# Expert tiles of 128 rows in place of 256, with three weight buffers and fetches three tiles ahead

## The chip, the core and the metric

The kernel runs on one core of a Trainium2 chip. The time is the device time of one execution in microseconds (us), from the first to the last instruction and what lies around them; a median of several runs is given. The profile is one execution recorded by the hardware profiler. Its engines are TensorE (PE for its matmuls, PEld for its weight loads), VectorE (DVE), ScalarE (ACT), GpSimd (POOL) and SyncE (SP), which here only issues transfers.

## What is computed

Two stages: attention between a sequence and a small state, per batch and head, and then a mixture of experts in which each of the 4352 rows goes to the one expert with the highest logit. Everything is float32.

```python
def _attn_ref(x, state):            # x (8, 8, 512, 64), state (8, 8, 32, 64)
    ...
    xread = np.matmul(a, state)     # a: softmax over the states
    ...
    sread = np.matmul(a2, x)        # a2: softmax over the tokens
    return np.concatenate([xread, sread], axis=2)

def _moe_ref(x, w_gate, w1, w2):    # x (4352, 512), w1 (8, 512, 1024), w2 (8, 1024, 512)
    logits = x @ w_gate
    expert_idx = np.argmax(logits, axis=1)
    ...
    for e in range(E):
        mask = expert_idx == e
        ...
        xe = x[mask]
        h = np.maximum(xe @ w1[e], 0.0)
        ye = h @ w2[e]
        out[mask] = gate_w[mask, None] * ye
```

## The kernel before

**Attention and routing** (up to about 214 us) goes over the eight batches. `route` (line 231) finds each row's expert and its rank there, and an indirect DMA of GpSimd (line 274) scatters the rows of x, each with its gate weight and its token number, into `xs_dram`, where every expert has a region of its own. Then VectorE computes tables (lines 344 to 388): for each tile the expert's number `eidx`, the rows of `xs_dram` to fetch `grow`, and which of its rows hold no token `inv_i`.

**Experts.** The rows of each expert are cut into tiles of T = 256 rows. A program has a fixed number of tiles, JT (line 49), enough for any split of 4352 rows over 8 experts: 24. All of them run, whatever the counts are; a tile past the last one fetches no rows, but does all the rest. The four steps of a tile j:

- `fetch(j)` (line 396): per 128 rows an indirect gather of GpSimd into one of six buffers `xg`; SP reads the expert's number and issues the loads of its w1 (2 MB) and w2 (2 MB) into `w1t` and `w2t`, tiles of `wpool` with two buffers each.
- `x_in(j)` (line 412): per 128 rows four transposes on TensorE into a PSUM tile `ptx`, evicted into `fxT` by ScalarE and VectorE in turn; VectorE also copies the gate weights `gw` and makes the row numbers `ti` of the output.
- `up(j)` (line 428): h = relu(x w1), with the weights as the stationary and `fxT` as the moving operand, 256 columns wide. Four PSUM tiles `ph` of 2 x 256 columns are evicted into `hT`, by ScalarE and VectorE in turn.
- `down(j)` (line 443): y = h w2, with `hT` stationary and 512 columns of w2 moving, once per 128 rows; VectorE multiplies by the gate weight into `y`, and an indirect DMA of GpSimd (line 452) scatters `y` into the output by `ti`.

The loop (line 462) writes up(j), x_in(j+1), down(j), fetch(j+2) for each j. From that a scheduler makes the order of each engine's instructions, and puts gathers and transposes whose buffers are free ahead of the first `up`. An engine takes its instructions in order, and waits on semaphores where an operand isn't ready or a buffer isn't free. So w1 of tile j+2 leaves when up(j) has read the last of its buffer, w2 when down(j) has. `wpool` is taken at the start of the kernel (line 53), beside the attention's pool `att`, which is released (line 390) ahead of the experts' pool `ffn`.

Of the kernel before, what the change touches and what calls it, by code (L numbers as in the profile page):

```python
# [9 lines left out]
FP32 = mybir.dt.float32  # L10
# [3 lines left out]
ALU = mybir.AluOpType  # L14
# [5 lines left out]
def kernel(  # L20
# [17 lines left out]
    SCALE = 0.125  # L38
    SO = S + NS                 # rows of one batch in the seam's token order
    NTOK = B * SO  # L40
    NC = S // 128               # token chunks of a batch; token s = 4 * p + c
    NPR = H // 2                # pairs of heads, 128 rows of (head, d)
    NDC = DM // 128
    NFC = F // 128
    XW = DM + 2                 # a routed row: x, gate weight, token number
    T = 256                     # tokens of one expert tile
    NH = T // 128
    # every split of NTOK tokens over E experts fits: sum of ceil(n_e / T)
    JT = (NTOK + E * (T - 1)) // T

    const = ctx.enter_context(tc.tile_pool(name="const", bufs=1))
    dram = ctx.enter_context(tc.tile_pool(name="dram", bufs=1, space=bass.MemoryType.DRAM))
    wpool = ctx.enter_context(tc.tile_pool(name="wpool", bufs=2))
    ps_m = ctx.enter_context(tc.tile_pool(name="ps_m", bufs=4, space=bass.MemoryType.PSUM))
    ps_o = ctx.enter_context(tc.tile_pool(name="ps_o", bufs=2, space=bass.MemoryType.PSUM))
    ps_s = ctx.enter_context(tc.tile_pool(name="ps_s", bufs=2, space=bass.MemoryType.PSUM))

    # expert e's rows start at e * NTOK, so that any split of the tokens fits
    xs_dram = dram.tile([E * NTOK, XW], I32)

# [1 line left out]
    ident = const.tile([128, 128], FP32)  # L62
# [7 lines left out]
                   allow_small_or_imprecise_dtypes=True)  # L70
    # 0/1 matrices and the one-hot rows are exact in bfloat16, and their products are counts
    U128 = const.tile([128, 128], BF16)
# [18 lines left out]

    # token numbers: batch b, chunk c, partition p -> b * SO + 4 * p + c
    tok_x = const.tile([128, B, NC], I32)
    nc.gpsimd.iota(tok_x[:], pattern=[[SO, B], [1, NC]], base=0, channel_multiplier=NC)
    # state rows of batches 4g..4g+3: partition 32 * i + n -> (4g + i) * SO + S + n
    quad = const.tile([128, 1], FP32)
# [13 lines left out]
    XB = 6  # L110
    # rows past an expert's count are not fetched: the buffers hold zeros or earlier rows there
    xg_bufs = []
# [7 lines left out]
    def evict(dst, src):  # L120
        """PSUM to SBUF, the two engines that can read PSUM in turn."""
        turn[0] += 1
        if turn[0] % 2:
            nc.scalar.copy(dst, src)  # L124
        else:
            nc.vector.tensor_copy(out=dst, in_=src)  # L126

    # =========================== attention and routing ===========================
    att = tc.alloc_tile_pool(name="att", bufs=2)

    # block-diagonal states: rows (h % 4, n), columns (h % 4, d), and their transposes by pairs
    bd = att.tile([128, B, 2, 4, D], FP32, bufs=1)
# [16 lines left out]
    def prep_state(b):  # L149
        pt = ps_m.tile([128, 2, 2, 128], FP32, tag="m", name="pt")  # L150
        for j in range(NPR):
            nc.tensor.transpose(pt[:, j // 2, j % 2, :], bd[:, b, j // 2, ts(j % 2, 2), :], ident[:])
        for i in range(2):
            evict(stT[:, b].rearrange("p (g i) n -> p g i n", i=2)[:, :, i, :], pt[:, :, i, ts(i, 2 * NS)])
        # state @ w_gate, by heads: the routing logits are the attention weights times it
        pg = ps_s.tile([128, 2, E], FP32, tag="s", name="pg")
        for j in range(NPR):
            nc.tensor.matmul(pg[ds(64 * (j % 2), 64), j // 2, :], lhsT=stT[:, b, j, :], rhs=wg[:, j, :],
                             start=True, stop=True, skip_group_check=True)
        evict(gst[:, b], pg[:])  # L160
# [10 lines left out]
    def read_weights(b, xT):  # L171
        """softmax over the states for every token"""
        a = att.tile([128, NC, H, NS], FP32, tag="a", name="a")
# [18 lines left out]
    def transpose_read(a):  # L192
        """rows (h % 4, n), columns tokens"""
        aT = att.tile([128, 2, NC, 128], FP32, tag="aT", name="aT")
        for g in range(2):
            pt = ps_m.tile([128, NC, 128], FP32, tag="m", name="pt")
            for c in range(NC):
                nc.tensor.transpose(pt[:, c, :], a[:, c, ts(g, 4), :], ident[:])
            evict(aT[:, g], pt[:])
        return aT  # L200

    def write_weights(b, xT):
        """softmax over the tokens for every state: rows (h % 4, n)"""
        a2 = att.tile([128, 2, S], FP32, tag="a2", name="a2")
# [16 lines left out]
    def transpose_write(a2):  # L221
        """rows tokens, columns (h % 4, n)"""
        a2T = att.tile([128, 2, NC, 128], FP32, tag="a2T", name="a2T")
        for g in range(2):
            pt = ps_m.tile([128, NC, 128], FP32, tag="m", name="pt")
            for c in range(NC):
                nc.tensor.transpose(pt[:, c, :], a2[:, g, ts(c, 128)], ident[:])
            evict(a2T[:, g], pt[:])
        return a2T

    def route(lg, row, tok, U):
        """lg: logits [128, U, E]; row: [128, U, XW] with x in place; sends each row to its expert's rows"""
        mx = att.tile([128, U, 1], FP32, tag="r_mx", name="r_mx")
        nc.vector.tensor_reduce(mx[:, :, 0], lg, AX.X, ALU.max)
        sh = att.tile([128, U, E], FP32, tag="r_sh", name="r_sh")
        nc.vector.tensor_tensor(sh[:], lg, mx[:].to_broadcast([128, U, E]), ALU.subtract)
        # the first expert among those at the maximum
        cand = att.tile([128, U, E], FP32, tag="r_cand", name="r_cand")
# [5 lines left out]
        nc.vector.tensor_tensor(oh[:], cand[:], m2[:].to_broadcast([128, U, E]), ALU.is_equal)  # L244
        # gate weight: exp(0) over the sum
        ex = att.tile([128, U, E], FP32, tag="r_ex", name="r_ex")
# [5 lines left out]
        nc.vector.tensor_copy(out=row[:, :, DM + 1:DM + 2].bitcast(I32), in_=tok.unsqueeze(2))  # L252
        # rank among the tokens of the same expert so far
        of = oh[:].rearrange("p u e -> p (u e)")
# [27 lines left out]
    def read_rows(b, aT):  # L282
        """x rows of the batch's tokens and their logits"""
        row = att.tile([128, NC, XW], FP32, tag="row", name="row")
# [15 lines left out]
    def write_rows(b, a2T):  # L300
        """x rows of the batch's states; those of four batches are routed together"""
        g4, r = b // 4, ds(NS * (b % 4), NS)
# [39 lines left out]

    # ============== tables: each tile's expert, its rows, and which of them are real ==============
    cnt = const.tile([128, E], FP32)
# [17 lines left out]
    nc.vector.tensor_copy(out=eidx[:], in_=ej[:])  # L362
    # the tile's number within its expert
    gt = const.tile([128, JT, E], FP32)
# [4 lines left out]
    nc.vector.tensor_scalar(loc[:], loc[:], float(T), iota_p[:, 0:1], ALU.mult, ALU.add)  # L369
    # the expert's count of tokens; far below zero for a tile past the last  # L370
    dcnt = const.tile([128, E], FP32)
# [19 lines left out]

    # ================================= experts =================================
    ffn = tc.alloc_tile_pool(name="ffn", bufs=2)
# [18 lines left out]
    def x_in(j):  # L412
# [3 lines left out]
        for k in range(NH):  # L416
# [4 lines left out]
            evict(xT[:, :, ts(k, 128)], pt[:])  # L421
            # no output row for a row that is not real: its token number is out of bounds
            nc.vector.tensor_tensor(ti[:, k:k + 1], xg[:, DM + 1:DM + 2].bitcast(I32),  # L423
# [4 lines left out]
    def up(j):  # L428
        xT, w1t = fs[j]["xT"], fs[j]["w1t"]
        hT = ffn.tile([128, NFC, T], FP32, tag="hT", name="hT")  # L430
        for f2 in range(NFC // 2):
            ph = ps_m.tile([128, 2, T], FP32, tag="m", name="ph")
            for i in range(2):
                for c in range(NDC):
                    nc.tensor.matmul(ph[:, i, :], lhsT=w1t[:, c, ts(2 * f2 + i, 128)], rhs=xT[:, c, :],  # L435
                                     start=(c == 0), stop=(c == NDC - 1), skip_group_check=True)
            if f2 % 2:
                nc.vector.tensor_scalar(hT[:, ts(f2, 2), :], ph[:], 0.0, None, ALU.max)  # L438
            else:
                nc.scalar.activation(hT[:, ts(f2, 2), :], ph[:], AF.Relu)  # L440
        fs[j]["hT"] = hT
# [17 lines left out]
    fetch(0)  # L459
    fetch(1)  # L460
    x_in(0)
    for j in range(JT):
        up(j)
        if j + 1 < JT:
            x_in(j + 1)
        down(j)
        if j + 2 < JT:
            fetch(j + 2)

    ffn.release()  # L470


# [28 lines left out]
```

## Time and profile before

| | |
|---|---|
| median of 3 runs | 931.94 us (928.96 to 932.76) |
| span of the profiled execution, first to last instruction | 925.5 us |
| mean granted TensorE clock | 0.979 of full speed |
| moved by DMA | 137.06 MB, 148 GB/s over the span |
| weight loads | 24 of w1 and 24 of w2, 2048.0 KB each |

No other time is recorded for the profiled execution than its span; the runs' median is 6.4 us above it. In the rows below, busy times are sums over an engine's instructions. Matmuls are pipelined, so the time of one is longer than the distance from one start to the next, and a price is read from starts. "idle before <- X" names what ended the idle time of the engine ahead of a group.

### The profile page before, as it was taken

The page shows a single profiled execution, that of the slowest core. Times are in us where ns is not written, and L with a number is a line of the kernel's source. Part 1 is how long each engine was busy: PE and PEld are TensorE (multiplying, and loading weights), DVE is VectorE, ACT ScalarE, POOL GpSimd, SP SyncE. Part 2 cuts the span into 40 slices and gives each one's busy share as a digit, 9 for nine tenths or more (in the row PEclk, how much of TensorE's full clock was granted, in tenths as well). Part 3 has the DMA queues.
Part 4 walks back from the last instruction along what each step waited for, and adds up shares of the span by engine and source line. Part 5 has one row for each costly group of instructions (what it writes and reads, how often), then busy time and mean ns, then how long its engine had stood idle before and what let it go on. Part 6 is the DMA issues. An engine that isn't in the chain of part 4 may idle for free.

```text
span 925.5 us, 9941 instructions
## 1 busy us (share of the span) xinstructions
PE 868.1 (94%) x4028; PEld 609.1 (66%) x4028; DVE 219.8 (24%) x628; ACT 99.4 (11%) x196; POOL 156.4 (17%) x166
## 2 busy tenths in 40 slices
PE   2999999990999999999999999999999999999997
PEld 2777877780766677666677666776667766667764
DVE  4456666543111111111111111111111111111110
ACT  1223322220100000000000000000000000000000
POOL 3022332224201111011110111111111101100000
PEclk9899999995799999999999999999999999999999
DMA  9034343117754464554544535545446435355300
GB/s 159 1 84 101 93 103 92 47 47 266 268 204 165 168 215 143 198 186 148 208 171 164 215 128 204 202 136 196 153 160 216 153 146 184 112 196 178 110 0 1
DMA packets 84061, 137.06 MB, mean 148 GB/s; under 512 B 40622, under 2 KB 40622, under 8 KB 84016
## 3 DMA queue, kind: packets, MB, share of 16 engines
q1 hardware_dynamic: 70912, 109.06, 36.5%
q0 software_dynamic: 10400, 26.83, 7.7%
q10 hardware_dynamic: 2704, 0.54, 0.4%
q8 instruction: 32, 0.52, 0.2%
q14 instruction: 13, 0.11, 0.0%
HBM read 122.22 MB, written 21.53 MB: 155 GB/s over the span
## 4 chain that ended last, share of the span: by engine, by line
issue 64%; POOL 9%; PE 3%; DMA 1%; POOLq 1%; DVE 0%
POOL out_dram L452 5%; POOL xg L398 3%; PE ph L435 2%; DMA xg<-xs_dram,grow 1%; PE py L448 1%; POOL xs_dram L274 0%; POOLq L398 0%; POOLq L452 0%; POOLq L496 0%; PE ptx L420 0%; DVE y L451 0%
## 5 line engine op out<-in xcount | busy, mean ns | idle before, releaser
L435 PE MATMUL ph<-fxT,w1t 128*128 128x256 f32 x1536 | 337.4, 381 | 0.0
L448 PE MATMUL py<-w2t,hT 128*128 128x512 f32 x768 | 333.6, 592 | 0.0
L435 PEld LDWEIGHTS ph<-fxT,w1t 128*128 128x128 f32 x1536 | 293.2, 191 | 50.1 <-issue 11.0
L448 PEld LDWEIGHTS py<-w2t,hT 128*128 128x128 f32 x768 | 144.2, 190 | 172.3 <-issue 172.2
L452 POOL DMA_INDIRECT out_dram<-y,ti x48 | 48.6, 1012 | 355.5 <-DVE y L451 323.9
L451 DVE TENSOR_SCALAR y<-py,gw 128x512 f32<-128x512 f32 x48 | 36.0, 751 | 293.6 <-PE py L448 293.6
L398 POOL DMA_INDIRECT xg<-xs_dram,grow x48 | 49.5, 1030 | 252.6 <-PE ptx L420 236.8
L440 ACT ACTIVATE hT<-ph 128x512 f32<-128x512 f32 x48 | 28.7, 597 | 553.0 <-PE ph L435 553.0
L438 DVE TENSOR_SCALAR hT<-ph 128x512 f32<-128x512 f32 x48 | 33.1, 690 | 145.9 <-PE ph L435 145.9
L420 PE MATMUL ptx<-ident,xg 128*128 128x128 f32 x192 | 27.7, 288 | 22.8 <-DMA xg<-xs_dram,grow 22.8
L274 POOL DMA_INDIRECT xs_dram<-row,r_sli x32 | 31.7, 992 | 81.7 <-DVE r_sli L271 30.2
L423 DVE TENSOR_TENSOR ti<-xg,inv_i 128x1 int32<-128x1 int32 x48 | 6.0, 158 | 164.8 <-DMA out_dram<-y,ti 143.0
L420 PEld LDWEIGHTS ptx<-ident,xg 128*128 128x128 f32 x192 | 23.6, 148 | 26.6 <-issue 22.8
L178 PE MATMUL pc<-stT,xT 128*128 128x64 f32 x256 | 37.2, 307 | 0.4 <-ACT stT L124 0.4
L178 PEld LDWEIGHTS pc<-stT,xT 128*128 128x128 f32 x256 | 34.9, 219 | 2.3 <-issue 1.4
L288 PE MATMUL px<-bd,aT 128*128 128x256 f32 x128 | 31.9, 387 | 0.1
L308 PE MATMUL pw<-x_nat,a2T 128*32 128x64 f32 x512 | 30.5, 219 | 0.0
L308 PEld LDWEIGHTS pw<-x_nat,a2T 128*32 128x32 f32 x512 | 28.8, 110 | 1.5 <-ACT r_ex L247 1.3
L189 POOL TENSOR_TENSOR a<-sh,sm 128x512 f32<-128x512 f32 x16 | 16.9, 1059 | 74.9 <-DVE sm L188 73.9
L167 PE MATMUL pt<-ident,x_nat 128*128 128x128 f32 x128 | 20.7, 300 | 7.4 <-DMA x_nat<-in_x_dram 6.8
L288 PEld LDWEIGHTS px<-bd,aT 128*128 128x128 f32 x128 | 22.7, 191 | 3.3 <-DVE aT L126 0.6
L124 ACT COPY fxT<-ptx 128x512 f32<-128x512 f32 x24 | 14.0, 585 | 98.3 <-PE ptx L420 98.3
(121 smaller groups left out, 391.0 us busy)
## 6 DMA issues: line engine op xcount, KB each, us to landing
w1t<-in_moe_w_dram SPq DMA_DIRECT2D x24, 2048.0 KB, 8.9
w2t<-in_moe_w_dram SPq DMA_DIRECT2D x24, 2048.0 KB, 9.1
x_nat<-in_x_dram SPq DMA_DIRECT2D x32, 256.0 KB, 5.1
xg<-xs_dram,grow POOLq DMA_INDIRECT x48, 6.9
out_dram<-y,ti POOLq DMA_INDIRECT x48, 3.1
bd<-in_state_dram ACTq DMA_DIRECT2D x8, 64.0 KB, 4.5
xs_dram<-row,r_sli POOLq DMA_INDIRECT x32, 5.2
xs_dram<-srow,r_sli POOLq DMA_INDIRECT x2, 6.1
```

What stands on the lines that cost most here:

```text
L178: nc.tensor.matmul(pc[:, i, ts(j, 2), :], lhsT=xT[:, j, 2 * u + i, :], rhs=stT[:, b, j, :], start=True, stop=True, skip_group_check=True)
L274: d = nc.gpsimd.indirect_dma_start(out=xs_dram[:], out_offset=bass.IndirectOffsetOnAxis(ap=sli[:, u:u + 1], axis=0), in_=row[:, u, :].bitc ...
L288: nc.tensor.matmul(px[:, ts(g, 256)], lhsT=aT[:, g, c, :], rhs=bd[:, b, g], start=True, stop=True, skip_group_check=True)
L308: nc.tensor.matmul(px[r, ts(h, D)], lhsT=a2T[:, h // 4, c, ts(h % 4, NS)], rhs=x_nat[b][:, c, h, :], start=(c == 0), stop=(c == NC - 1), s ...
L398: nc.gpsimd.indirect_dma_start(out=xg_bufs[(NH * j + k) % XB][:].bitcast(I32), out_offset=None, in_=xs_dram[:], in_offset=bass.IndirectOff ...
L420: nc.tensor.transpose(pt[:, c, :], xg[:, ts(c, 128)], ident[:])
L435: nc.tensor.matmul(ph[:, i, :], lhsT=w1t[:, c, ts(2 * f2 + i, 128)], rhs=xT[:, c, :], start=(c == 0), stop=(c == NDC - 1), skip_group_chec ...
L438: nc.vector.tensor_scalar(hT[:, ts(f2, 2), :], ph[:], 0.0, None, ALU.max)
L440: nc.scalar.activation(hT[:, ts(f2, 2), :], ph[:], AF.Relu)
L448: nc.tensor.matmul(py[:], lhsT=hT[:, f, ts(k, 128)], rhs=w2t[:, f, :], start=(f == 0), stop=(f == NFC - 1))
L451: nc.vector.tensor_scalar(y[:], py[:], gw[:, k:k + 1], None, ALU.mult)
L452: d = nc.gpsimd.indirect_dma_start(out=out[:], out_offset=bass.IndirectOffsetOnAxis(ap=ti[:, k:k + 1], axis=0), in_=y[:], in_offset=None, ...
```

## The change

T becomes 128. Three things follow in the code without an edit: NH = T // 128 is 1, so that a tile has one gather, one group of transposes, one product `py` and one scatter; JT becomes (4352 + 8 x 127) // 128 = 41; and the tables are made for 41 tiles. `up` forms its PSUM tiles from FB = 512 // T = 4 pieces of 128 columns, so that an eviction still covers 128 x 512 elements, and there are two per tile. `wpool` gets three buffers, and is taken after the attention's pool is released, so that it lies in memory that attention used. The loop fetches three tiles ahead. The six `xg` buffers hold six tiles in place of three. Comments were taken out, which is left out here.

```diff
-    T = 256                     # tokens of one expert tile
+    T = 128
     NH = T // 128
...
-    wpool = ctx.enter_context(tc.tile_pool(name="wpool", bufs=2))
...
     att.release()

+    wpool = tc.alloc_tile_pool(name="wpool", bufs=3)
     ffn = tc.alloc_tile_pool(name="ffn", bufs=2)
...
         hT = ffn.tile([128, NFC, T], FP32, tag="hT", name="hT")
-        for f2 in range(NFC // 2):
-            ph = ps_m.tile([128, 2, T], FP32, tag="m", name="ph")
-            for i in range(2):
+        FB = 512 // T
+        for f2 in range(NFC // FB):
+            ph = ps_m.tile([128, FB, T], FP32, tag="m", name="ph")
+            for i in range(FB):
                 for c in range(NDC):
-                    nc.tensor.matmul(ph[:, i, :], lhsT=w1t[:, c, ts(2 * f2 + i, 128)], rhs=xT[:, c, :],
+                    nc.tensor.matmul(ph[:, i, :], lhsT=w1t[:, c, ts(FB * f2 + i, 128)], rhs=xT[:, c, :],
...
             if f2 % 2:
-                nc.vector.tensor_scalar(hT[:, ts(f2, 2), :], ph[:], 0.0, None, ALU.max)
+                nc.vector.tensor_scalar(hT[:, ts(f2, FB), :], ph[:], 0.0, None, ALU.max)
             else:
-                nc.scalar.activation(hT[:, ts(f2, 2), :], ph[:], AF.Relu)
+                nc.scalar.activation(hT[:, ts(f2, FB), :], ph[:], AF.Relu)
...
     fetch(0)
     fetch(1)
+    fetch(2)
     x_in(0)
...
-        if j + 2 < JT:
-            fetch(j + 2)
+        if j + 3 < JT:
+            fetch(j + 3)

     ffn.release()
+    wpool.release()
```

TensorE's order in the middle of the expert loop, one tile and the start of the next, before (`ph` is written by up, `ptx` by the transposes of a later tile, `py` by down; a row is a run of products of the code, each two instructions in the trace except the transposes; numbers behind a name tell its buffers apart):

```order
L435 MATMUL ph_2629<-fxT_2568,w1t_2523 128x256 x8
L435 MATMUL ph_2639<-fxT_2568,w1t_2523 128x256 x8
L435 MATMUL ph_2649<-fxT_2568,w1t_2523 128x256 x8
L435 MATMUL ph_2659<-fxT_2568,w1t_2523 128x256 x8
L420 MATMUL ptx_2672<-ident_73,xg4_127 128x128 x4
L420 MATMUL ptx_2680<-ident_73,xg5_129 128x128 x4
L448 MATMUL py_2688<-w2t_2525,hT_2628 128x512 x8
L448 MATMUL py_2702<-w2t_2525,hT_2628 128x512 x8
```

The same place after, two tiles:

```order
L436 MATMUL ph_2719<-fxT_2683,w1t_2570 128x128 x16
L436 MATMUL ph_2737<-fxT_2683,w1t_2570 128x128 x16
L420 MATMUL ptx_2758<-ident_70,xg2_120 128x128 x4
L449 MATMUL py_2766<-w2t_2572,hT_2718 128x512 x8
L436 MATMUL ph_2791<-fxT_2755,w1t_2642 128x128 x16
L436 MATMUL ph_2809<-fxT_2755,w1t_2642 128x128 x16
L420 MATMUL ptx_2830<-ident_70,xg3_122 128x128 x4
L449 MATMUL py_2838<-w2t_2644,hT_2790 128x512 x8
```

A tile keeps its 32 products of up, at half the width, and has half the transposes and half the products of down; the sequence of the steps is the same.

The first weight loads on SP, before, with what they wait for (DMAHW and DMASW are the semaphores of transfers that SP or ScalarE, and GpSimd, issued):

```order
L403 TENSOR_LOAD eidx_2146 [waits DVE_49]
L407 DMA w1t_2188<-in_moe_w1_dram 128x4x1024 [waits DMAHW1_49]
L409 DMA w2t_2190<-in_moe_w2_dram 128x8x512 [waits DMAHW2_49]
L407 DMA w1t_2201<-in_moe_w1_dram 128x4x1024 [waits DMAHW3_49]
L409 DMA w2t_2203<-in_moe_w2_dram 128x8x512 [waits DMAHW4_49]
L407 DMA w1t_2321<-in_moe_w1_dram 128x4x1024 [waits DMAHW5_49,DMAHW1_49,PE_49]
```

And after:

```order
L403 TENSOR_LOAD eidx_2143 [waits DVE_49]
L407 DMA w1t_2179<-in_moe_w1_dram 128x4x1024 [waits DMASW6_49,DMASW7_49,DMASW5_49,DMAHW0_49,DMASW4_49,DMAHW1_49,DMASW3_49,DMAHW2_49,DMASW2_49,DMAHW3_49,DMASW1_49,DMAHW4_49,DMASW0_49,DMAHW5_49,DVE_49,DMAHW6_49,PE_49,DMAHW7_49,Activation_4
L409 DMA w2t_2181<-in_moe_w2_dram 128x8x512
L407 DMA w1t_2189<-in_moe_w1_dram 128x4x1024
L409 DMA w2t_2191<-in_moe_w2_dram 128x8x512
L407 DMA w1t_2199<-in_moe_w1_dram 128x4x1024
L409 DMA w2t_2201<-in_moe_w2_dram 128x8x512
L407 DMA w1t_2282<-in_moe_w1_dram 128x4x1024 [waits DMAHW1_49,PE_49]
```

The first load has moved behind everything that used the attention's memory, the scatters into `xs_dram` included; it is the first load of tile 3, and no longer that of tile 2, that waits for TensorE to free a buffer.

VectorE's order in the middle of the loop, one tile, before (`hT` is an eviction of up, `y` one of down; `ti` and `gw` belong to a later tile):

```order
L438 TENSOR_SCALAR hT_2426<-ph_2437 128x512 [waits PE_49,Activation_49]
L438 TENSOR_SCALAR hT_2426<-ph_2457 128x512 [waits PE_49]
L126 COPY fxT_2467<-ptx_2478 128x4x128 [waits PE_49]
L451 TENSOR_SCALAR y_2495<-py_2486,gw_2368 128x512 [waits PE_49]
L451 TENSOR_SCALAR y_2509<-py_2500,gw_2368 128x512 [waits PE_49]
L425 COPY gw_2772<-xg0_119 128x1 [waits DMASW2_49,DVE_49]
L425 COPY gw_2772<-xg1_121 128x1 [waits DMASW3_49]
L423 TENSOR_TENSOR ti_2771<-xg0_119,inv_i_2162 128x1 [waits DMASW5_49,DMASW4_49]
```

And after, two tiles:

```order
L439 TENSOR_SCALAR hT_2646<-ph_2665 128x512 [waits PE_49,Activation_49]
L125 COPY fxT_2683<-ptx_2686 128x512 [waits PE_49]
L452 TENSOR_SCALAR y_2703<-py_2694,gw_2613 128x512 [waits PE_49]
L425 COPY gw_2901<-xg4_124 128x1 [waits DMASW7_49,DVE_49]
L423 TENSOR_TENSOR ti_2900<-xg4_124,inv_i_2159 128x1 [waits DMASW6_49]
L439 TENSOR_SCALAR hT_2718<-ph_2737 128x512 [waits PE_49,Activation_49]
L452 TENSOR_SCALAR y_2775<-py_2766,gw_2685 128x512 [waits PE_49]
```

The wait of `ti` for the scatter of the tile whose slot it takes (the DMASW semaphore in its row) stands between y of one tile and hT of the next in both, but a tile has one eviction of hT by VectorE in place of two.

## Rows read from the trace of the kernel before

**Rows 1.** The page, busy time of each engine, its share, instructions

```profile
PE 868.1 (94%) x4028; PEld 609.1 (66%) x4028; DVE 219.8 (24%) x628; ACT 99.4 (11%) x196; POOL 156.4 (17%) x166
```

**Rows 2.** Windows: the expert loop and its start; the first row names columns

```profile
core 0: us, PE busy (x) PEld busy (x) DVE busy (x) ACT busy (x) POOL busy (x), PEclk, DMA share, GB/s
...
238.20:920.40 682.20, 682.20 (x2479) 456.89 (x2477) 91.69 (x204) 41.53 (x70) 87.31 (x86) 1.00 0.46 163
...
218.00:246.00 28.00, 12.69 (x46) 9.95 (x47) 3.08 (x18) 1.77 (x3) 10.09 (x10) 0.57 1.02 389
```

**Rows 3.** Timeline of TensorE, one tile: start, length, engine, line, operation, count

```profile
523.29 13.98 PE L435 MATMUL ph<-fxT,w1t 128*128 128x256 f32 x64
537.10 1.04 PE L420 MATMUL ptx<-ident,xg 128*128 128x128 f32 x8
537.97 13.90 PE L448 MATMUL py<-w2t,hT 128*128 128x512 f32 x32
551.71 0.59 PE L435 MATMUL ph<-fxT,w1t 128*128 128x256 f32 x2
```

**Rows 4.** Groups of instructions of the experts: busy, mean ns | idle before

```profile
L435 PE MATMUL ph<-fxT,w1t 128*128 128x256 f32 x1536 | 337.4, 381 | 0.0
L448 PE MATMUL py<-w2t,hT 128*128 128x512 f32 x768 | 333.6, 592 | 0.0
...
L420 PEld LDWEIGHTS ptx<-ident,xg x192: 139/141/231, 231.7 to 878.8; 128*128 128x128 f32 x192
```

**Rows 5.** Weight loads with 64 and 8 columns: timeline, single durations (min/median/max)

```profile
64.18 3.34 PE L178 MATMUL pc<-stT,xT 128*128 128x64 f32 x28
...
64.18 3.20 PEld L178 LDWEIGHTS pc<-stT,xT 128*128 128x128 f32 x28
...
208.19 1.06 PE L320 MATMUL pls<-wg,sT 128*128 128x8 f32 x8 [0.56 <-DVE sT L126]
...
208.19 0.97 PEld L320 LDWEIGHTS pls<-wg,sT 128*128 128x128 f32 x8 [0.65 <-DVE sT L126]
...
L178 PEld LDWEIGHTS pc<-stT,xT x256: 186/192/338, 22.6 to 179.8; 128*128 128x128 f32 x128
```

**Rows 6.** Weight loads, w1t then w2t: issue to landing

```profile
DMA to landing us min/median/max: 7.6/8.9/25.4
...
DMA to landing us min/median/max: 8.3/9.1/26.0
```

**Rows 7.** Start of the loop: timeline; last row the scatters from 209 us on

```profile
214.61 0.39 SPq L407 DMA_DIRECT2D w1t<-in_moe_w_dram  x1
...
215.47 0.98 POOL L274 DMA_INDIRECT xs_dram<-srow,r_sli  x1 [0.30 <-issue]
...
224.42 1.05 POOL L398 DMA_INDIRECT xg<-xs_dram,grow  x1 [7.96 <-issue]
...
231.75 1.08 PE L420 MATMUL ptx<-ident,xg 128*128 128x128 f32 x4 [21.23 <-DMA xg<-xs_dram,grow]
...
237.66 0.87 PE L420 MATMUL ptx<-ident,xg 128*128 128x128 f32 x3 [0.37 <-DMA xg<-xs_dram,grow]
...
238.32 15.92 PE L435 MATMUL ph<-fxT,w1t 128*128 128x256 f32 x64
...
DMA to landing us min/median/max: 3.2/3.6/8.2
```

**Rows 8.** A scatter of the output and VectorE: timeline; scatters' landing times

```profile
523.49 0.75 DVE L451 TENSOR_SCALAR y<-py,gw 128x512 f32<-128x512 f32 x1 [6.12 <-PE py L448]
...
524.52 1.00 POOL L452 DMA_INDIRECT out_dram<-y,ti  x1 [5.84 <-DVE y L451]
...
530.76 0.23 DVE L423 TENSOR_TENSOR ti<-xg,inv_i 128x1 int32<-128x1 int32 x2 [6.28 <-DMA out_dram<-y,ti]
530.91 0.69 DVE L438 TENSOR_SCALAR hT<-ph 128x512 f32<-128x512 f32 x1
...
DMA to landing us min/median/max: 2.1/3.1/8.1
```

## The prediction

> **What bounds the kernel now.** I read the share of busy time first, then the windows, then the timeline of one expert tile. TensorE is busy for 94% of the span [rows 1]. The windows say where: from 238.2 to 920.4 us, the whole expert loop, it is busy 682.2 of 682.2 us at a granted clock of 1.00, that is 2.4 GHz, while the DMA engines are busy 46% of the time and move 163 GB/s [rows 2]. So 74% of the span is a loop that no other engine and no transfer delays, and its length is what TensorE is given to do.
>
> The timeline of one tile gives the prices [rows 3]. up(j) starts at 523.29, the transposes of a later tile at 537.10, down(j) at 537.97 and the next up at 551.71: 13.81 us for 64 matmuls of 256 columns (0.2158 us each), 0.87 us for 8 transposes of 128 columns (0.109 each), 13.74 us for 32 matmuls of 512 columns (0.4294 each), together 28.42 us; 24 of them are 682.1 us. An fp32 product is two instructions in the trace: a tile of `up` has 8 x 4 products in the code and 64 in the rows [rows 3, 4]. Each streams 0.84 ns per column, so the time of `up` and `down` is rows times columns; a row that holds no token costs as much as one that does.
>
> **What the change does to TensorE.** JT (line 49) falls from 24 tiles of 256 rows to 41 of 128: 6144 rows become 5248. Per tile `up` keeps its 64 instructions, since each still needs its own 128 x 128 piece of w1, but each streams 128 columns; `down` falls from 32 to 16 instructions of 512 columns; the transposes from 8 to 4. As the change's order shows, `up`, `x_in` and `down` follow each other as before, and four of the 41 groups of transposes now stand ahead of the loop.
>
> The one unknown price is an fp32 matmul of 128 columns with its own fp32 weights; this trace has none. The nearest rows: 28 loads and 28 matmuls of 64 columns in a row at full clock [rows 5]. One load lasts 0.192 us, 28 span 3.20, so they start (3.20 - 0.192) / 27 = 0.111 us apart. With 8 columns it is (0.97 - 0.192) / 7 = 0.111 again [rows 5]. The number of columns did not matter between 8 and 64, so a load takes 0.111 us of its own and the matmul of 64 columns (about 0.055 us) lies wholly beside it. In `up` the load is hidden the other way: 0.2158 us is the price of the columns alone. At 128 columns the load is 0.111 and the columns are 0.109 (the transposes, [rows 3]). If they overlap as on both sides of this width, the price is the larger one, a little rounded up: 0.112. The ends are 0.109 (only the columns count) and 0.221 (load and columns one after the other). I take 0.112, since both neighbouring rows show full overlap.
>
> The sum, for the loop:
> - before: 1536 x 0.2158 = 331.5; 768 x 0.4294 = 329.8; 173 of the 192 transposes (19 come ahead of the loop, the first four and last three of five groups in [rows 7]) x 0.109 = 18.9. Together 680.2 us, and with some 2 us lost to a clock of 1.2 GHz in the first `up` (15.92 us where the others take 13.98, [rows 3, 7]) this is the window's 682.2.
> - after: 41 x 64 = 2624 x 0.112 = 293.9; 41 x 16 = 656 x 0.4294 = 281.7; (164 - 16) x 0.109 = 16.1. Together 591.7 us, 14.47 us per tile.
> - difference: -88.5 us. `up` gives 37.6 of it, `down` 48.1, the transposes 2.8.
>
> **What hides the rest.** The weights are fetched per tile, so 41 x 4.19 MB where it was 24 x 4.19. Per tile of 14.47 us the DMA engines now move 4.19 MB of weights, 0.26 MB of gathered rows (128 x 514 x 4 B) and 0.26 MB of output, 4.72 MB. At the start of the loop, with much queued, they moved 389 GB/s at a busy share of 1.02 [rows 2]: 4.72 MB take 12.1 us, 84% of the tile. The weights thus stay hidden, with 2.4 us to spare per tile. w1 of tile j+3 is asked for when up(j) ends and needed at up(j+3), some 36 us later; a load lands 8.9 or 9.1 us after its issue in the median [rows 6]. SP's queue holds nothing but these loads, so a late one delays only its successors.
>
> VectorE: after y(j) it waits for the scatter of tile j before it rewrites that tile's `ti` slot, and only then evicts the second half of hT. Before, the scatter left 1.23 us after down's end, landed 6.2 us later, and hT's eviction came at 530.91, half a microsecond late, for nobody [rows 8]. Now that eviction is asked for 7.2 us after down's end, and TensorE wants it only after the transposes and half of down, at 7.17 + 0.44 + 8 x 0.4294 = 11.05 us. The chain is 1.23 + landing + 0.23 (`ti`) + 0.69 (hT) + some 0.1: it fits as long as the landing takes under 8.8 us. The longest in the trace is 8.1 [rows 8]. So nothing is charged. ScalarE, GpSimd (two indirect DMAs of 1 us per tile in place of four) and the one transposed eviction per tile are far off the path.
>
> **The start.** Before, wpool lay apart from the attention's tiles, and w1 of tile 0 left at 214.61, before the last scatter into xs_dram. Now wpool is taken after `att.release()`, and SP's first load waits for all eight semaphores of the scatters. That sounds like a loss. But the loop starts when the first groups of gathered rows are transposed: TensorE does five groups from 231.75 on, one every 1.47 us, and up(0) begins at 238.32 [rows 7]. Their first gather left at 224.42, held by the last scatter, which left at 215.47 and took 8.2 us to land while 8 MB of weights were moving; others landed in 3.2 to 3.6 [rows 7]. Without weights in the way it should land at 219 to 223.7, so the gathers leave 0 to 4.6 us earlier, and one group fewer stands ahead of up(0): -1.5 to -6.1 us. Against that the weights leave 5 to 9 us later: w1(0), some 9 us after an issue at 220 to 224 [rows 6], lands at 229 to 233, shortly before it is needed, and sharing the DMA engines with the gathers may make it some us late. I take -4, with -6 and +2 as ends.
>
> **The sum.** Span 925.5 - 88.5 - 4 = 833.0 us. The runs' median is 931.94, 6.4 above the profiled span; I keep that: 839.4 us. With 0.109 per matmul the time would be 831.5, and with -6 at the start besides 829.5. The end of the program (the last y, its scatter, its landing) is unchanged.
>
> **Rivals.**
> - **The load of w1 is not hidden at 128 columns** (ends slower). Load and columns are nearly equal here, so any gap between them shows, 2624 times. With half the load uncovered the price is 0.109 + 0.056 = 0.165: + 2624 x 0.053 = +139, 978 us. It decides at 0.112 + 92.5 / 2624 = 0.147 us: above that the change is a loss. For it speaks that no row has both at full size (the transposes' loads are shorter, a median of 0.141 us a piece [rows 4] against 0.192 [rows 5]). Against it speak the two full overlaps in [rows 3] and [rows 5]. Chance 6%, and 4% for something between 0.12 and 0.147 (860 to 930 us).
>  The Trainium skill, page "TensorE: Matmul & The Clock Gate", section "Back-to-back issue gap", speaks against this change: it says that in a stream of weight load and matmul pairs both set the spacing, and gives about 81 ns at 128 columns where the columns alone would take about 56. By that ratio, 1.45, an estimate for this kernel would be 0.158 us and some 960 us. The trace contradicts it at 8 and 64 columns, and no row shows 128 with this load.
> - **The transfers become the bound.** If two loads do not overlap, a tile costs their two landing times, 8.9 + 9.1 = 18.0 us [rows 6]: 41 x 18.0 = 738, +146, 986 us. It decides at 14.47 + 92.5 / 41 = 16.7 us per tile, 283 GB/s. Against it: 389 GB/s over 28 us with loads queued [rows 2], and two loads can always be outstanding now. Chance 2% for slower than before, 4% for a tile of 15 to 16 us (860 to 900).
> - **The scatter's landing.** With the DMA engines 84% busy it may take longer than the 8.8 us that are free; each further microsecond stops TensorE for one per tile. At 10 us: 1.2 x 41 = 49, 889 us. Chance 6%.
> - That the change doesn't do what it says is excluded: JT is fixed when the program is built, and its order holds 41 pairs of weight loads.
>
> **Chances.** The forecast 78%; the others as above. About 0.5% is the least that a measurement of this kernel tells from no change. Faster 0.91, same 0.01, slower 0.08. The range goes from 827 (0.109 and the better start are 829.5, and the runs themselves differ by 2 us to either side) over the forecast's own upper end, some 853 (0.115 and the worse start), to 880, to take in the milder of the partial stalls.
>
> **What would show it.** Right: `up` of 64 matmuls in 7.1 to 7.2 us, a tile of 14.4 to 14.5, TensorE busy throughout the loop at clock 1.00, DMA share 0.8 to 0.9 at some 325 GB/s, up(0) at 232 to 237. Wrong: starts of LDWEIGHTS in `up` more than 0.12 us apart (the load shows); idle time of TensorE ahead of the first `ph` or `py` put down to a weight load (transfers); idle time in the middle of `py` put down to hT and a `ti` that ends over 10 us after down's end (the scatter).

## The result and the profile after

The changed kernel takes 833.48 us in the median of four runs (830.12 to 840.71) against 930.61 us (928.96 to 932.76) of the kernel before beside it: a ratio of 0.897, 95% interval 0.891 to 0.903. 839.4 us was predicted, range 827 to 880. The profiled execution is the longest of the four, 840.71 us with a span of 838.9.

The page's busy times of the changed kernel (beside [rows 1]):

```profile
PE 788.4 (94%) x4976; PEld 594.1 (71%) x4976; DVE 205.3 (24%) x591; ACT 93.5 (11%) x186; POOL 142.4 (17%) x152
```

The share of TensorE is the old one; the time that it is busy fell by 80 us. The windows, beside [rows 2] (columns as there; the first row is the start of the loop):

```profile
240.00:260.00 20.00, 19.62 (x109) 15.38 (x110) 2.56 (x8) 1.18 (x2) 3.48 (x4) 0.89 1.03 392
300.00:400.00 100.00, 100.00 (x586) 73.79 (x585) 14.13 (x32) 5.94 (x10) 14.45 (x14) 1.00 0.99 360
500.00:600.00 100.00, 100.00 (x587) 73.85 (x586) 14.14 (x32) 5.94 (x10) 14.46 (x14) 1.00 0.93 324
700.00:800.00 100.00, 100.00 (x587) 73.91 (x586) 13.78 (x30) 5.94 (x10) 9.07 (x9) 1.00 0.86 304
```

Behind the first tile TensorE has no idle time in the loop and its granted clock is 1.00 (2.4 GHz); the transfers doubled to some 320 GB/s, and SP's loads still wait for TensorE to free their buffers. One tile on the timeline, TensorE (beside [rows 3]), then VectorE and GpSimd (beside [rows 8]), the landing times of the 21 scatters from 400 to 700 us, and VectorE's longest wait at `ti` in the loop:

```profile
502.44 7.31 PE L436 MATMUL ph<-fxT,w1t 128*128 128x128 f32 x64
502.64 0.75 DVE L452 TENSOR_SCALAR y<-py,gw 128x512 f32<-128x512 f32 x1 [5.13 <-PE py L449]
503.67 1.01 POOL L453 DMA_INDIRECT out_dram<-y,ti  x1 [6.61 <-DVE gw L425]
509.58 0.60 PE L420 MATMUL ptx<-ident,xg 128*128 128x128 f32 x4
510.02 7.03 PE L449 MATMUL py<-w2t,hT 128*128 128x512 f32 x16
511.54 0.16 DVE L423 TENSOR_TENSOR ti<-xg,inv_i 128x1 int32<-128x1 int32 x1 [7.96 <-DMA out_dram<-y,ti]
511.62 0.69 DVE L439 TENSOR_SCALAR hT<-ph 128x512 f32<-128x512 f32 x1
516.89 7.31 PE L436 MATMUL ph<-fxT,w1t 128*128 128x128 f32 x64
...
DMA to landing us min/median/max: 6.5/7.7/8.3
...
382.26 0.16 DVE L423 TENSOR_TENSOR ti<-xg,inv_i 128x1 int32<-128x1 int32 x1 [8.73 <-DMA out_dram<-y,ti]
```

From start to start: `up` 7.14 us (0.1116 per instruction), transposes 0.44, `down` 6.87 (0.4294), the tile 14.45. VectorE stands 7.96 us at `ti` until the scatter lands and ends hT at 512.31; TensorE reads that half of hT at 510.02 + 8 x 0.4294 = 513.45. The wait is there in 37 of the 41 tiles; in this one it is 1.1 us short of costing anything. It comes nearer: the longest landing of the loop is 8.6 us, VectorE's wait for it ends at 382.26, hT at 383.03, and that tile's `down`, which starts at 379.97, reads this half of hT at 383.41, 0.4 us later.

The start, beside [rows 7]: the last scatter of the routing, the first load of w1, the first gather, the first transposes, up(0), the first `down`:

```profile
226.14 0.98 POOL L273 DMA_INDIRECT xs_dram<-srow,r_sli  x1 [0.30 <-issue]
229.90 0.39 SPq L407 DMA_DIRECT2D w1t<-in_moe_w_dram  x1
230.33 1.05 POOL L398 DMA_INDIRECT xg<-xs_dram,grow  x1 [3.22 <-issue]
237.30 1.08 PE L420 MATMUL ptx<-ident,xg 128*128 128x128 f32 x4 [16.06 <-DMA xg<-xs_dram,grow]
241.91 8.47 PE L436 MATMUL ph<-fxT,w1t 128*128 128x128 f32 x64
250.72 7.11 PE L449 MATMUL py<-w2t,hT 128*128 128x512 f32 x16 [0.34 <-DMA w2t<-in_moe_w_dram]
```

From the last scatter to up(0) are 15.8 us, before 22.85: -7.1. That scatter itself is 10.7 us later than in [rows 7], in attention code that did not change. The clock tells why. The same run of products, and the clock around it, first of the kernel before, then of the changed one:

```profile
60.00:70.00 10.00, 9.59 (x82) 7.46 (x79) 4.66 (x9) 2.53 (x5) 4.09 (x4) 1.00 0.90 194
67.45 1.94 PE L209 MATMUL pc<-xT,stT 128*64 128x512 f32 x8
```

```profile
70.00:80.00 10.00, 9.32 (x52) 5.97 (x51) 7.30 (x21) 3.62 (x8) 2.12 (x2) 0.82 0.14 34
70.02 3.68 PE L208 MATMUL pc<-xT,stT 128*64 128x512 f32 x8
```

The 8 matmuls take 1.94 us at a granted clock of 1.00 and 3.68 where it falls to 0.50 for a while. With the 28 ahead of them (line 178, now 177) it is 5.14 us from start to end before and 8.37 after, and the same happens to two more batches: 9.7 of the 10.7 us. The time varies between executions of one kernel (spans of the changed one: 828.4 to 838.9, the longer ones mostly at a lower mean clock), so no part of the result is read from the attention stage.

### The profile page after: what moved, and what is told of

It is laid out like the page before. It is cut to its first block, busy times and chain, and to the rows that moved or that the text cites. A ratio compares the mean times of both kernels' runs of the same rounds, so it can differ in the third digit from the quotient of the medians.

```text
span 838.9 us, 11936 instructions
## 1 busy us (share of the span) xinstructions
PE 788.4 (94%) x4976; PEld 594.1 (71%) x4976; DVE 205.3 (24%) x591; ACT 93.5 (11%) x186; POOL 142.4 (17%) x152
## 4 chain that ended last, share of the span: by engine, by line
PE 63%; issue 6%; DMA 3%; POOL 1%; POOLq 0%; DVE 0%; SPq 0%
PE ph L436 31%; PE py L449 30%; DMA w2t<-in_moe_w_dram 2%; PE ptx L420 2%; POOL out_dram L453 0%; DMA xs_dram<-srow,r_sli 0%; POOLq L499 0%; POOL xs_dram L273 0%; DVE y L452 0%; SPq L407 0%; DVE gw L425 0%; POOLq L453 0%; SPq L409 0%
## 5 line engine op out<-in xcount | busy, mean ns | idle before, releaser
L436 PEld LDWEIGHTS ph<-fxT,w1t 128*128 128x128 f32 x2624 | 300.6, 193 | 19.1 <-issue 19.1
L436 PE MATMUL ph<-fxT,w1t 128*128 128x128 f32 x2624 | 300.8, 276 | 0.0
L449 PE MATMUL py<-w2t,hT 128*128 128x512 f32 x656 | 288.4, 592 | 0.3 <-DMA w2t<-in_moe_w_dram 0.3
L449 PEld LDWEIGHTS py<-w2t,hT 128*128 128x128 f32 x656 | 121.4, 190 | 137.8 <-issue 135.3
L453 POOL DMA_INDIRECT out_dram<-y,ti x41 | 41.3, 1008 | 339.8 <-DVE gw L425 270.6
L452 DVE TENSOR_SCALAR y<-py,gw 128x512 f32<-128x512 f32 x41 | 30.8, 751 | 202.9 <-PE py L449 202.9
L398 POOL DMA_INDIRECT xg<-xs_dram,grow x41 | 42.7, 1041 | 185.6 <-PE ptx L420 179.0
L177 PE MATMUL pc<-stT,xT 128*128 128x64 f32 x256 | 43.6, 342 | 0.4 <-ACT stT L123 0.4
L177 PEld LDWEIGHTS pc<-stT,xT 128*128 128x128 f32 x256 | 41.1, 252 | 2.3 <-issue 1.4
L208 PE MATMUL pc<-xT,stT 128*64 128x512 f32 x64 | 26.0, 855 | 0.0
```

Of the source, the lines that this page charges most:

```text
L177: nc.tensor.matmul(pc[:, i, ts(j, 2), :], lhsT=xT[:, j, 2 * u + i, :], rhs=stT[:, b, j, :], start=True, stop=True, skip_group_check=True)
L208: nc.tensor.matmul(pc[ts(i, 64), :], lhsT=stT[:, b, j, :], rhs=xT[:, j], start=True, stop=True, skip_group_check=True)
L398: nc.gpsimd.indirect_dma_start(out=xg_bufs[(NH * j + k) % XB][:].bitcast(I32), out_offset=None, in_=xs_dram[:], in_offset=bass.IndirectOff ...
L436: nc.tensor.matmul(ph[:, i, :], lhsT=w1t[:, c, ts(FB * f2 + i, 128)], rhs=xT[:, c, :], start=(c == 0), stop=(c == NDC - 1), skip_group_che ...
L449: nc.tensor.matmul(py[:], lhsT=hT[:, f, ts(k, 128)], rhs=w2t[:, f, :], start=(f == 0), stop=(f == NFC - 1))
L452: nc.vector.tensor_scalar(y[:], py[:], gw[:, k:k + 1], None, ALU.mult)
```

## The experiments

A time and that of the kernel before beside it are of one chip; on the chips of e8 to e12 the kernel before took 941 to 942 us, on the others 931 to 933. So ratios are compared.

**e1: which part pays.** The smaller tile with the old pool, two buffers, two tiles ahead: in the kernel before, only

```
-    T = 256                     # tokens of one expert tile
+    T = 128
```

and the FB of `up`.

> The tile of 128 rows alone: two weight buffers taken at the start of the kernel and fetches two tiles ahead, as before the change. Theory (the smaller tile is the whole gain in the loop, two buffers would hide the loads too): a tile of 14.45 us and a loop of 592 us as in the changed kernel; only the start differs, since the weights leave ahead of the last scatters again: last scatter to the first up 21.4 us in place of 15.8, so some 839 us where the changed kernel has 833.5. Rival (the third buffer carries part of the gain): TensorE idle ahead of ph or py for a load, 1 us or more per tile, 875 us or more.

Measured: 834.77 us, ratio 0.900 (0.892 to 0.907); 839 was expected. TensorE is as full as with three buffers, the DMA engines busy 90%:

```profile
500.00:600.00 100.00, 100.00 (x580) 73.22 (x579) 14.14 (x32) 5.95 (x10) 14.46 (x14) 1.00 0.90 323
```

From the last scatter to up(0) it takes 21.8 us, 1.1 less than before. The tile height alone gives nearly the whole gain, and the third buffer hides nothing that two leave open.

**e2: the other two parts alone.** In the changed kernel `T = 128` becomes `T = 256`.

> The other two parts alone: tiles of 256 rows, three weight buffers taken after the attention's memory is released, fetches three tiles ahead. Theory: the loop stays at 24 x 28.42 = 682 us, and the start is 5.6 us shorter than in the kernel before (last scatter to the first up 17.3 us in place of 22.9, with five groups of transposes ahead): 925 us. Rival (later weights cost more at the start than the earlier gathers give): 931 us or more.

Measured: 927.07 us, ratio 0.995 (0.991 to 0.999). Its start:

```profile
221.73 0.98 POOL L273 DMA_INDIRECT xs_dram<-srow,r_sli  x1 [0.30 <-issue]
225.88 1.04 POOL L398 DMA_INDIRECT xg<-xs_dram,grow  x1 [3.17 <-issue]
...
239.49 13.98 PE L436 MATMUL ph<-fxT,w1t 128*128 128x256 f32 x64
```

And the landing times of the last five scatters of the routing, in e1 (weights already moving), then in e2:

```profile
DMA to landing us min/median/max: 3.2/3.3/8.8
```

```profile
DMA to landing us min/median/max: 3.2/3.4/3.7
```

Last scatter to first gather 4.15 us (before 8.95), to up(0) 17.8 (before 22.85). That is the effect of the late pool: with no weights moving, the last scatter lands sooner (8.2 us before [rows 7] and 8.8 in e1, at most 3.7 in e2 and 3.6 in the changed kernel). The medians differ by 5.5 us. In this trace the loop is also 2.5 us shorter, 1.9 of them because up(0) takes 13.98 us in place of 15.92 [rows 7]: its clock is 1.00 here, and whether that belongs to the change one trace cannot settle. -5.1 from e2 and -1.1 from e1 make -6.2 of the -7.1.

**e5: 1 MB more for every tile.** Behind the load of w1t:

```
+        xtra = wpool.tile([128, NDC // 2, F], FP32, tag="xtra", name="xtra")
+        nc.sync.dma_start(out=xtra[:], in_=moe_w1[ds(e, 1)].rearrange("o (c p) f -> p (o c) f", p=128)[:, 0:NDC // 2])
```

> The changed kernel with 1 MB more fetched per tile (the first half of w1 once more, into a buffer that nobody reads): 5.77 MB per tile in place of 4.72. Theory A (the transfers can run at the 389 GB/s seen with much queued, 16% of a tile is to spare): 14.8 us per tile, TensorE waits 0.2 to 0.4 us per tile, 840 to 850 us. Theory B (the busy share of 0.92 at 324 GB/s in the middle of the loop is the measure, 353 GB/s is the limit and 8% is to spare): 16.3 us per tile, 910 us.

Measured: 837.97 us, ratio 0.898 (0.894 to 0.902):

```profile
500.00:600.00 100.00, 100.00 (x586) 73.48 (x586) 13.61 (x31) 6.54 (x11) 14.46 (x14) 1.00 1.04 400
```

What TensorE waited for in the loop, from 240 to 830 us:

```profile
PE ph L438 <- DMA w1t<-in_moe_w_dram: 1.2, 2, 0.7
PE py L451 <- DMA w2t<-in_moe_w_dram: 0.4, 1, 0.4
```

The DMA engines move 400 GB/s at a busy share of 1.04, 5.77 MB in the time of a tile, and TensorE waits for a load three times in the whole loop, 1.6 us together. Theory B falls; theory A had the waits larger than they are, 840 to 850 us. The loads stay just ahead, with nothing to spare: e9 moves no more per second.

**e9: 2 MB more** (`NDC` in place of `NDC // 2`).

> The changed kernel with 2 MB more fetched for every tile (w1 a second time into a buffer that nothing reads): 6.82 MB a tile. Theory A (TensorE bounds the changed kernel by a small margin, and the transfers bind as soon as they take longer than its 14.45 us): with 1 MB more, 5.77 MB a tile, the queues moved 397 to 400 GB/s and TensorE still had no idle time; at 398 GB/s 6.82 MB take 17.1 us, 2.7 us more than the tile, so the time goes to 833.5 + 41 x 2.7 = 944 us (930 to 960), TensorE waits for w1t or w2t in every tile, and the granted clock may fall after such waits. Theory B (there is more room in the transfers than 400 GB/s): under 850 us.

Measured: 944.24 us, ratio 1.004 (1.001 to 1.007). At a base of 930.61, from which the 944 of the expectation was reckoned, that is 934 us, inside its range; that the figures agree to the microsecond is luck, since this chip is slower. The window, and what TensorE waited for from 300 to 700 us:

```profile
300.00:400.00 100.00, 85.73 (x485) 61.22 (x484) 12.33 (x27) 4.74 (x8) 12.40 (x12) 1.00 1.04 399
```

```profile
PE ph L438 <- DMA w1t<-in_moe_w_dram: 47.3, 21, 2.9
```

The DMA rate is the same as in e5; now `up` waits for w1t 21 times, in most tiles. The prediction's rival that the transfers become the bound is real, and it begins at about 1 MB more per tile, where e5 has its first waits.

**e3: is a 128-column instruction paid by its load?** `up` streams 64 columns; the second half of h is a copy of the first (ScalarE's eviction is cut in two in the same way):

```
-  nc.tensor.matmul(ph[:, i, :], ..., rhs=xT[:, c, :],
+  nc.tensor.matmul(ph[:, i, 0:64], ..., rhs=xT[:, c, 0:64],
-  nc.vector.tensor_scalar(hT[:, ts(f2, FB), :], ph[:], 0.0, None, ALU.max)
+  for q in range(2):
+      nc.vector.tensor_scalar(hT[:, ts(f2, FB), ts(q, 64)], ph[:, :, 0:64], 0.0, None, ALU.max)
```

> The changed kernel, but each matmul of up streams 64 columns in place of 128, and the second half of each tile's rows of h is a copy of the first (half of up's work is left out). The weight loads stay as they are. Theory (at 128 columns the fp32 weight load of 0.111 us already sets the pace): up stays at 7.1 us and the time within 1% of 833. Rival (the columns set it): 64 x 0.056 = 3.6 us for up; the transfers then hold a tile at 12.1 to 13.3 us, so 740 to 790 us.

Measured: 957.3 us, ratio 1.024 (1.014 to 1.033). No theory had that. The timeline:

```profile
506.97 7.25 PE L436 MATMUL ph<-fxT,w1t 128*128 128x64 f32 x64
508.20 1.03 POOL L455 DMA_INDIRECT out_dram<-y,ti  x1 [6.72 <-DVE gw L425]
515.58 0.16 DVE L423 TENSOR_TENSOR ti<-xg,inv_i 128x1 int32<-128x1 int32 x1 [7.47 <-DMA out_dram<-y,ti]
515.66 0.76 DVE L440 TENSOR_SCALAR hT<-ph 128x256 f32<-128x256 f32 x2
516.34 0.68 DVE L125 COPY fxT<-ptx 128x512 f32<-128x512 f32 x1
517.12 1.08 PE L420 MATMUL ptx<-ident,xg 128*128 128x128 f32 x4 [2.90 <-issue]
518.00 8.04 PE L451 MATMUL py<-w2t,hT 128*128 128x512 f32 x16
```

The question is answered by the first row: with half the columns `up` lasts 7.25 us in place of 7.31, 0.111 per instruction in place of 0.1116, so its price is that of the loads. The rest is a new wait. The order of the instructions is set when the program is built, and with this edit the transposes of a tile four ahead, no longer those of the next one, stand between `up` and `down`, behind the copy that frees their PSUM buffer; that copy stands on VectorE behind hT, hT behind `ti`, and `ti` behind the landing of a scatter. "issue" in the last bracket of TensorE hides it: the transposes begin 0.1 us after the copy's end. From 300 to 700 us:

```profile
PE ptx L420 <- issue: 36.6, 12, 3.4
PE ptx L420 <- ACT fxT L123: 7.9, 11, 0.7
```

3.05 us where VectorE copies, 0.7 where ScalarE does. And the clock falls behind the long waits:

```profile
514.00:516.00 2.00, 0.22 (x3) 0.09 (x1) 0.42 (x2) 0.00 (x0) 0.00 (x0) 1.00 0.92 328
516.00:518.00 2.00, 0.88 (x5) 0.91 (x5) 1.02 (x3) 0.00 (x0) 1.04 (x1) 0.65 0.93 334
518.00:520.00 2.00, 2.00 (x4) 0.97 (x4) 0.00 (x0) 0.00 (x0) 0.00 (x0) 0.50 1.03 424
520.00:522.00 2.00, 2.00 (x5) 0.80 (x5) 0.00 (x0) 0.00 (x0) 0.00 (x0) 1.00 0.99 400
```

**e8: the same with eight buffers of `ti` and `gw`** (`bufs=4` becomes `bufs=8`).

> The 64-column kernel again (up streams 64 of the 128 columns, and the second half of h is a copy of the first), with eight buffers of ti and gw in place of four and nothing else moved. In the 64-column kernel the transposes waited 12 times for 36.6 us (3.05 us each) between 300 and 700 us where VectorE had its turn to copy fxT, and 11 times for 7.9 us (0.7 us each) where ScalarE had it; VectorE's copy stood behind hT, hT behind ti, and ti behind the landing of a scatter. Theory A (that scatter is the cause): with eight ti VectorE no longer stands at ti, its hT (0.75 us) and its copy (0.68 us) end about 1.6 us after up, the wait falls from 3.05 to 1.2 to 1.9 us and the time falls by 20 turns x 1.2 to 1.9 us and by what the half clock cost after them, to 880 to 930 us. Theory B (the wait has nothing to do with the scatter): the wait stays at 3 us on VectorE's turns and the time at 957 us.

Measured: ratio 1.015 (1.006 to 1.024), no different from e3. But the edit did not take the wait away (from 300 to 700 us the transposes wait 3.05 us each on VectorE's turns, as in e3), so it tells nothing on theory A:

```profile
510.29 0.16 DVE L423 TENSOR_TENSOR ti<-xg,inv_i 128x1 int32<-128x1 int32 x1 [7.33 <-DMA out_dram<-y,ti]
```

The order built computes `ti` as far ahead as its buffers let it, three tiles with four buffers and seven with eight, and so always into the buffer of the scatter that has just left.

**e11: a `ti` for each tile** (`bufs=JT`), in the 64-column kernel.

> The 64-column kernel (up streams 64 of the 128 columns, and the second half of h is a copy of the first) with a ti and a gw of its own for each of the 41 tiles. With eight buffers the wait of VectorE at ti stayed (7.33 us, ended by the landing of the scatter issued just before), because the order built with eight buffers computes ti seven tiles ahead in place of three: ti goes as far ahead as its buffers let it, and so it always takes the buffer of the scatter just issued. With 41 buffers no ti shares one with a scatter, and in the order built ti stands behind hT and behind the copy of fxT. Theory A (the wait of the transposes comes from the scatter, by way of ti, hT and the copy): on VectorE's turns the transposes wait 1.3 to 2.0 us in place of 3.05, on ScalarE's turns 0.7 us as before; the time falls by some 20 x 1.1 us and what the half clock cost, to 0.94 to 1.00 of the kernel before (1.0148 to 1.0236 measured for the other two). Theory B (it comes from elsewhere): still 3 us, and 1.015 to 1.024 of the kernel before.

Measured: 918.75 us, ratio 0.977 (0.969 to 0.985):

```profile
PE ptx L420 <- issue: 18.6, 12, 1.6
PE ptx L420 <- ACT fxT L123: 8.7, 12, 0.7
```

1.55 us in place of 3.05, and only where the scatter stood in the chain: theory A. So 1.5 us of each long wait came from the scatter. What stays is the edit's own chain, hT and the copy.

**e12: a `ti` for each tile in the changed kernel.**

> The changed kernel with a ti and a gw of its own for each of the 41 tiles and nothing else. In the changed kernel VectorE waits 7.96 us for the landing of the scatter in every tile, and TensorE never waits for VectorE: hT ends at 512.31 us and is read at 513.45 us. Theory A (that wait is cover and costs nothing): no change, a ratio of 0.89 to 0.905 to the kernel before, and in the trace hT of the second half starts within 0.2 us of the end of up instead of 2 us behind it. Theory B (the wait costs something that the profile doesn't show): under 0.885.

Measured: 839.15 us, ratio 0.895 (0.888 to 0.903), no change:

```profile
507.39 0.60 PE L420 MATMUL ptx<-ident,xg 128*128 128x128 f32 x4
507.65 0.69 DVE L439 TENSOR_SCALAR hT<-ph 128x512 f32<-128x512 f32 x1 [5.47 <-issue]
```

hT comes 0.3 us after `up` in place of 2.0 (0.2 was expected), and TensorE gains nothing. The risk that a slow scatter holds hT up is gone. VectorE has not stopped waiting for a landing, though: `ti` now waits as long for the gather of a later tile, with y behind it:

```profile
515.64 0.16 DVE L423 TENSOR_TENSOR ti<-xg,inv_i 128x1 int32<-128x1 int32 x1 [6.70 <-DMA xg<-xs_dram,grow]
515.78 0.74 DVE L452 TENSOR_SCALAR y<-py,gw 128x512 f32<-128x512 f32 x1
```

y starts some 0.9 us after `down` in place of 0.2, and TensorE has no idle time from 300 to 700 us: the wait has moved to a place with more cover.

**e10: three tiles fewer** (`JT = ... - 3`; 38 of the 41 hold rows with these inputs, so this is a measurement only).

> The changed kernel with 38 tiles in place of 41. With these inputs 38 tiles hold rows and the last three of the 41 hold none; for other inputs 41 can be needed, so it is a measurement and no replacement. Theory A (an empty tile costs TensorE what a full one does, 14.45 us): 833.5 - 3 x 14.45 = 790 us (785 to 795). Theory B (a tile without rows costs less, since no rows are gathered or scattered for it): over 800 us.

Measured: 809.82 us, ratio 0.860 (0.856 to 0.864), 800 us (797 to 804) at a base of 930.61; 790 was expected, 785 to 795. The price of theory A is right and its time is not: from the last scatter of the routing to the end of the last `down` are 565.1 us where the changed kernel has 608.4: -43.2, three tiles of 14.45 are 43.35. But from there to the end of the span it is 11.9 us in place of 4.4. The last scatter, here and in the changed kernel:

```profile
796.94 0.98 POOL L453 DMA_INDIRECT out_dram<-y,ti  x1 [13.03 <-DVE y L452]
```

```profile
835.58 0.98 POOL L453 DMA_INDIRECT out_dram<-y,ti  x1 [13.03 <-DVE y L452]
```

It leaves 10.8 us ahead of the span's end here and 3.3 there. Here it carries rows, there none; in the changed kernel the scatters of the last three tiles land in 2.1 us, those of the others in 6.4 to 8.6. So the likely cause is the landing of the rows; the landing itself is not told by this trace. Empty tiles at the end cost TensorE full price, and seem to hide the last landing.

## Why the prediction was right, point by point

- **TensorE bounds the loop before and after**: right. Idle time 0 in the windows above.
- **A 128-column instruction costs 0.112 us, load and columns overlapped**: right, 0.1116, and e3 shows that the load sets it. The rival that the load is not hidden (0.165) falls. The Trainium skill's page "TensorE: Matmul & The Clock Gate", section "Back-to-back issue gap", gives about 81 ns for a pair of load and matmul at this width where the columns alone would take about 56, by which an estimate is 1.45 times the columns. Here it is 0.1116 against 0.109, 1.02 times, and the measurement decides.
- **The loop, -88.5 us, 14.47 per tile**: 14.45 measured. From up(0) to the end of the last `down` 592.6 us; before, 682.1 (238.32 to 920.4 [rows 2, 7]): -89.5.
- **The transfers fit, 12.1 us a tile at 389 GB/s**: right in the verdict, at some 320 GB/s. The rate under load is even 400 GB/s (e5), so the margin was about 1 MB per tile in place of the 0.9 that 389 GB/s would give, and e9 shows the rival beyond it.
- **The scatter's landing, under 8.8 us**: right, but by little. With the DMA engines busy the median rose from 3.1 [rows 8] to 7.5 us, and the longest is 8.6. The prediction charged nothing on the word of the old landing times, which did not last; that all stayed under its bound is partly luck. In e3 the same chain, reordered, cost 1.5 us of each wait of 3.05 (e11), and the clock fell behind these waits.
- **The start, -4 with ends of -6 and +2**: -7.1, outside its ends. The mechanism was right (the gather leaves 4.8 us earlier after the last scatter, 4.15 against 8.95 us in e2), the size was not: the gather leaves 4.8 us earlier where 4.6 was the best end, from the gather to up(0) it is 2.3 us less where 1.5 was forecast for one group of transposes fewer, and I took 2 us off the better end for weights that might come late. The late weights cost one wait of 0.34 us for w2t.
- **The 6.4 us between span and time**: not what they were taken for, but harmless. In all runs the time is about 1.8 us more than the span; the other 4.6 say that the profiled execution before was shorter than the median one. Since the sum starts from that span and adds the 6.4 again, it is the median of 931.94 less 92.5. It missed the median by 5.9 us: 3.1 at the start, 1.0 in the loop, 1.3 because the kernel before measured 930.61 this time, and 0.5 that stays open and is less than runs of one kernel differ by.
- **Two loads can always be outstanding**, an argument against the transfers as the bound: not needed. e1 hides the loads with two buffers; the third gives nothing in the loop, the late pool some 5 us ahead of it.

## What to carry to other kernels

When the busy engine's work is rows times columns, count the rows that hold nothing first: smaller tiles pay until the fixed cost of an instruction (here its weight load, 0.111 us) is no longer covered by the columns it streams, and at 128 fp32 columns (0.109) the two are nearly equal. Then price what doubles (the loads per row) against the measured rate, and look for the in-order engine that stands at a landing: a wait that costs nothing here cost 1.5 us in every second tile after a reordering (e3, e11). More buffers do not remove such a wait if the builder's order uses them to run further ahead (e8); a buffer per tile took it off hT, and the engine stood at another landing instead (e12).

## What the runs showed of the hardware

- A load of fp32 weights and an fp32 matmul of equal length overlap fully: 0.1116 us per pair at 128 columns (0.111 the load, 0.109 the columns), 0.111 at 64 (e3).
- One core's transfers ran at 396 to 402 GB/s from 300 to 800 us (e9), above the 389 of [rows 2].
- An indirect scatter of 128 rows took 3.1 us to land with the DMA engines 46% busy (median, [rows 2, 8]) and 7.7 at a busy share of 0.93.
- TensorE's granted clock fell to 0.50 (1.2 GHz) towards the end of an idle time of 2.9 us (e3), was still there in the first 2 us of `down` and was back at 1.00 in the next two, with no gap in between; the 16 instructions took 8.04 us in place of 7.03. In e11, from 300 to 700 us, it fell after six of twelve waits of 1.55 us and after three of twelve of 0.73 or less; what tells these apart stays open.
